# Windowed attention with sinks, then a maxout FFN: order of first loads, two reordered stretches, and one more chunk transposed by DMA

## The chip, the cores and the metric

The kernel runs on one NeuronCore of a Trainium2 chip. The metric is the device time of one execution in microseconds (us); the time of a kernel is the median of several runs. Five engines run side by side, each with its own instruction order: TensorE (PE; its weight loads are shown as PEld), VectorE (DVE), ScalarE (ACT), GpSimd (POOL) and SyncE (SP), which here only issues DMAs. They wait for each other by semaphores.

## The reference

Inputs are q, k, v of shape (4, 8, 768, 64) = batch, heads, positions, head width. Attention is causal with a window of 128 positions, and the first four positions of each sequence (the sinks) can always be seen. The heads are joined to x of 3072 tokens by 512, and a feed-forward layer takes the largest of three products:

```python
keep = is_sink | in_window            # in_window: 0 <= query - key < 128; is_sink: key < 4
scores = np.where(keep, q @ k.T / 8, -1e9)
x = softmax(scores) @ v               # per batch and head, then heads joined: (3072, 512)
h = np.maximum(np.maximum(x @ w1, x @ w2), x @ w3)      # w1, w2, w3: (512, 768)
out = h @ w_out                                         # w_out: (768, 512)
```

Inputs and output are float32; the kernel computes in bfloat16 with float32 sums.

## The kernel before

The 3072 tokens are cut into 12 chunks of 256, three to a batch (`CPB` is 3). Chunks 0, 3, 6 and 9 begin a batch: they have no sinks outside their own window and so no sink products. One token of text such as `Fa3` is a step: a letter for the kind, a letter for which chunk, and an argument. `run` turns the texts into instructions in just this order, on all engines; nothing is reordered later. Each engine takes its own instructions in the order in which they were written. The kinds that matter here:

- `K`, `Q`: k or q of a chunk is transposed on TensorE (`prep`, L227; `prep_runs`, L240, for chunks 1 and 2) and copied out of PSUM, k by VectorE, q mostly by ScalarE. From chunk 4 on this is done by the DMA crossbar instead: `D` (`turn`, L262) puts two transposing DMAs on SP's queue, and `E` (`place_k`, L221) lays out k on VectorE.
- `L` loads a chunk's q, k and v through SP's queue (L59, L89); GpSimd casts them to bfloat16 (`cast`, L215).
- `S` (L291) makes the scores of one pair of heads on TensorE and the exponentials on ScalarE; `M` (L314) multiplies by the mask on VectorE. `B` opens score buffers for chunks 0 and 1. `Z` (L321) makes the scores of the sinks, `V` (L337) opens a chunk's four attention outputs with the sinks' share, `A` (L349) adds the window's share for one pair of heads, and VectorE normalises it into x.
- `T` (`xpose`, L371) turns one half of a chunk's x into xT: up to chunk 4 by four transposes on TensorE and a copy, from chunk 5 on by one DMA on SP's queue.
- `F` (`ffn_h`, L389) makes one of nine groups of h on TensorE: eight matmuls of 256 columns, then a ScalarE copy (the groups 0, 3, 6, first weight) or a VectorE maximum (the others). `Y` and `W` (`ffn_y`, L410) make the output of a half or of a whole chunk; ScalarE copies it out of PSUM and SP stores it.

All PSUM tiles come from one pool of eight buffers with one tag, so that each new tile takes over the buffer of an older one and waits for its last reader. The masks, the sink rows and a few small matmuls for warming (`warm`, L124) are set up first. `sink_v_init` (L178) is four GpSimd instructions, two memsets and two copies, which prepare constants for the sinks' v rows. The first weights come by GpSimd's DMA queue (`load_runs`, `load_v`, `load_w`, `load_wo`), those of chunk 0 by SP's.

Chunks 0 to 2 and the beginning of chunk 3 are written out by hand (L501 to L546). Then a loop over chunks (L548) writes one pass for each: the h groups of chunk i, with the attention of chunk i+1 between them, the turning of chunk i+3 and the load of chunk i+4, then the scores of chunk i+2 and the output of chunk i. The passes of chunks 2 and 3 had texts of their own; in chunk 2's pass the output is made inside it (`Ya0`, `Ya1`) and the `Wa0` at the end is left out.

Of the kernel before, what the change touches and what calls it, by code (L numbers as in the profile page):

```python
# [16 lines left out]
def kernel(  # L17
# [24 lines left out]
    CPB = S // 256  # L42
# [8 lines left out]
    with tc.manual_schedule():  # L51
# [26 lines left out]
        def load_runs(ci):  # L78

            b, c = divmod(ci, CPB)  # L80
            t0 = c * 256
            runs[ci] = raw.tile([128, 2, 16 * D], BF16, tag="runs", bufs=2, name="runs")
            for j, src in ((0, k), (1, q)):
                nc.gpsimd.dma_start(
                    out=runs[ci][:, j],
                    in_=src[b, :, t0:t0 + 256].rearrange("h (r x) d -> h r (x d)", x=16))
            raws[ci] = [None]
# [10 lines left out]
        def load(ci, gate=None):  # L98
            load_qk(ci, gate)
            load_v(ci)  # L100
# [23 lines left out]
        def warm(n):  # L124

            wp = psum.tile([128, 128], F32, tag="f", name="warm")
            for _ in range(n):
                nc.tensor.matmul(wp, lhsT=ident, rhs=ident, start=True, stop=True)  # L128
# [29 lines left out]
        def load_w(wi, lo=0, hi=d_ff):  # L158

            w = (moe_w1, moe_w2, moe_w3)[wi]  # L160
            wt = const.tile([128, DS, hi - lo], BF16, name=f"w{wi}_{lo}")
            nc.gpsimd.dma_start(out=wt, in_=w[:, lo:hi].rearrange("(a p) f -> p a f", p=128))
            for fb in range(lo // 128, hi // 128):
                w_sb[wi, fb] = wt[:, :, fb * 128 - lo:fb * 128 - lo + 128]
# [3 lines left out]
        def load_wo():  # L168
            for a in range(2):
                nc.gpsimd.dma_start(  # L170
                    out=wo[:, 3 * a:3 * a + 3],
                    in_=moe_w_out[384 * a:384 * a + 384].rearrange("(a p) f -> p a f", p=128))
# [5 lines left out]
        def sink_v_init():  # L178
            nc.gpsimd.memset(sel, 0.0)
            nc.gpsimd.memset(v_sink[:, :, D:D + 1], 1.0)  # L180
            idv = ident[0:R, 0:R].rearrange("r (s p h) -> r p s h", p=NP, h=2)
            for h in range(2):
                nc.gpsimd.tensor_copy(sel[:, h, :, 0:2 * n_sink].rearrange(
                    "r p (s h) -> r p s h", h=2)[:, :, :, h], idv[:, :, :, h])

        def sink_v():
            for h in range(2):
                pv = psum.tile([128, B, D + 1], F32, tag="f", name="vs_ps")
                nc.tensor.matmul(pv, lhsT=sel[:, h].rearrange("r p x -> r (p x)"), rhs=v_sink,
                                 start=True, stop=True)  # L190
                nc.vector.tensor_copy(vs[:, :, h], pv)
# [3 lines left out]
        def cast_qk(ci, j, g, eng):  # L195
            if ci not in bfs:
                bfs[ci] = raw.tile([128, 2, 2, 2, 256], BF16, tag="qk_bf", name="qk_bf")
            src = raws[ci][0][:, j, g].rearrange("p (h i d) -> p h i d", h=4, d=D)
            if ci <= CPB:
                dst = bfs[ci][:, j, g]  # L200
            else:
                dst = bfs[ci][:, j].rearrange("p i a x -> p i (a x)")[:, :, 256 * g:256 * g + 256]
            (eng.tensor_copy if eng else nc.scalar.copy)(  # L203
                dst.rearrange("p i (h d) -> p h i d", d=D), src)
# [10 lines left out]
        def cast(ci):  # L215
            for j, g in ((0, 0), (1, 0), (0, 1), (1, 1)):
                cast_qk(ci, j, g, nc.gpsimd)
            for n in range(2):
                cast_v(ci, n, nc.gpsimd)
# [151 lines left out]
        def xpose(ci, t):  # L371
            if t == 0:
                xTs[ci] = work.tile([128, 2, DS, 128], BF16, tag="xT", bufs=3, name="xT")
            if ci > CPB + 1:
                nc.sync.dma_start_transpose(
                    out=xTs[ci][:, t], in_=xs[ci][:, t].rearrange("p h d -> p (h d)"))
                return
            pt = psum.tile([128, DS, 128], BF16, tag="f", name="xt_ps")
            x = xs[ci][:, t].rearrange("p h d -> p (h d)")
            for ds in range(DS):  # L380
                nc.tensor.transpose(pt[:, ds], x[:, ds * 128:(ds + 1) * 128], ident)  # L381
            copy = nc.vector.tensor_copy if ci == 0 else nc.scalar.copy
            copy(xTs[ci][:, t], pt)  # L383
# [69 lines left out]
        def step(op):  # L453

            name, ci, arg = op[0], int(op[1:3]), op[3:]
            if ci >= NCH:
                return
            if name in "KQ":
                (prep_runs if ci in runs else prep)(ci, int(name == "Q"), int(arg))
            elif name == "D":  # L460
                turn(ci)
            elif name == "L":
                load(ci)
            elif name == "E":
                place_k(ci, kTs.pop(ci), slice(0, NP))
            elif name == "S":
                score(ci, [int(x) for x in arg])
            elif name == "B":
                score_banks(ci, [int(x) for x in arg])
            elif name == "M":  # L470
                mask(ci, [int(x) for x in arg])
            elif name == "Z":
                if ci % CPB:
                    sink_score(ci)
            elif name == "X":
                if ci % CPB == 0:
                    sink_k(ci // CPB)
            elif name == "V":
                if ci % CPB:
                    sink_av(ci)  # L480
            elif name == "A":
                av(ci, int(arg))
            elif name == "T":
                xpose(ci, int(arg))
            elif name == "F":
                ffn_h(ci, int(arg))
            elif name == "Y":
                ffn_y(ci, [int(arg)], [range(FB)])
            elif name == "W" and ci == NCH - 1:
                ffn_y_end(ci)  # L490
            elif name == "W":
                ffn_y(ci, [0, 1], [range(4), range(4, FB)])

        def run(text, **at):
            for tok in text.split():
                c = at[tok[1]]
                step(f"{tok[0]}{c:02d}{tok[2:]}")

        sink_v_init()  # L501
        load_runs(1)
        load_v(1, nc.gpsimd)
        load_w(0, 0, 256)
        load_w(0, 256, d_ff)
        warm(36)
        cast_qk(0, 0, 0, nc.vector)
        cast_qk(0, 1, 0, nc.vector)
# [18 lines left out]
        load_runs(2)  # L527
        load_v(2, nc.gpsimd)
        load_wo()
        warm(3)  # L530
        run("Aa0 Aa1 Aa2 Aa3 Kb0 Qb0 Ta0 Ta1 Bb01 Sb01 Zb", a=0, b=1)
        sink_v()
        run("Bb23 Sb23 Fa0 Vb Ab0 Ab1 Fa3 Ab2 Ab3 Fa6 Fa1 Tb0 Tb1 Fa4", a=0, b=1)
        cast_v(2, 0, nc.gpsimd)
# [3 lines left out]
            a=0, b=1, c=2)  # L538
# [1 line left out]
        nc.gpsimd.memset(ve[1][:, :, :, D:D + 1], 1.0)  # L540
        cast(3)
        load(4)
        run("Fb5 Sc23 Mc23 Vc Ac0 Fb8 Ac1 Ya0 Ya1", a=0, b=1, c=2)
        cast(4)
        run("Ac2 Ac3 Yb0 Tc0 Tc1 Kd0 Qd0 Yb1 Kd1 Qd1", b=1, c=2, d=3)
        run("Zd Sd0123 Md0123 De Lf", d=3, e=4, f=5)  # L546

        for i in range(2, NCH):  # L548
            if i + 3 < NCH:
                cast(i + 3)  # L550
            text = "Fa0 Fa1 {} Fa2 {} Zc Sc0123 Mc0123 Wa0"
            if i == 2:
                text = text.format("", "Vb Ab0 Fa3 Ab1 Xb Fa4 Ab2 Fa5 Ab3 Fa6 Dd Le Fa7 Fa8 Ya0 Ec Tb0 Tb1 Ya1")
                text = text.replace(" Wa0", "")
            elif i == CPB:
                text = text.format("Ec", "Fa3 Vb Ab0 Fa4 Ab1 Fa5 Ab2 Fa6 Ab3 Dd Le Fa7 Fa8 Tb0 Tb1")
            elif i < 0:
                text = text.format("Ec", "Vb Ab0 Fa3 Xb Ab1 Fa4 Ab2 Fa5 Ab3 Fa6 Dd Le Fa7 Tb0 Tb1 Fa8")
            else:
                text = text.format("Ec", "Vb Ab0 Fa3 Xb Ab1 Fa4 Ab2 Fa5 Ab3 Tb0 Tb1 Fa6 Dd Le Fa7 Fa8")  # L560
            run(text, a=i, b=i + 1, c=i + 2, d=i + 3, e=i + 4)
# [38 lines left out]
```

## Time and profile before

| | |
|---|---|
| median of 7 runs | 183.31 us (182.16 to 183.87) |
| the profiled execution | 182.86 us, of which the span on the engines is 180.8 us |
| TensorE busy | 170.4 us (94% of the span) |
| VectorE, ScalarE, GpSimd busy | 115.5, 90.2, 69.8 us |
| moved by DMA | 33.63 MB, mean 186 GB/s |
| granted TensorE clock | 1.00 |
| DMA issues of xT on SP's queue | 14, median 2.9 us from issue to landing |
| of kT and qT on SP's queue | 8 each, 4.0 and 3.2 us |

The profile is one execution recorded by the hardware. All its times are microseconds from the beginning of the span, and it names tiles as the program does (`h_ps` is h in PSUM, `y_ps` the output, `o_ps` the attention output, `st` scores, `sk` sink scores, `xt_ps` transposed x). A line of it gives the line of the program, the engine, the operation, and output <- inputs with their shapes. In the timeline a bracket at the end tells how long the engine had been idle before and what released it. The chain of waits follows the work that ended last backwards through whatever released it. Matmul durations include the depth of a pipeline, so the sum of the busy times of single matmuls is more than what they add to the engine's sequence.

### The profile page before, as it was taken

How to read it: one execution, taken by the hardware profiler on the slowest of the kernel's cores; microseconds unless marked ns; L12 is line 12 of the kernel's file. 1: busy time of each engine (PE TensorE's matmuls, PEld its weight loads, DVE VectorE, ACT ScalarE, POOL GpSimd, SP SyncE). 2: the span in 40 equal slices, each digit the busy share in tenths (PEclk: the TensorE clock that was granted, in tenths of full speed). 3: DMA queues.
4: the chain of work that ended last, by engine and by line, in shares of the span. 5: the costliest groups of instructions: out<-in, count | busy, mean ns of one | idle time of the engine just before them, and what ended most of it. 6: DMA issues, size and time to landing. Idle time of an engine off the chain costs nothing.

```text
span 180.8 us, 4873 instructions
## 1 busy us (share of the span) xinstructions
PE 170.4 (94%) x1974; PEld 131.6 (73%) x1985; DVE 115.5 (64%) x245; ACT 90.2 (50%) x191; POOL 69.8 (39%) x121
## 2 busy tenths in 40 slices
PE   6869989999999999999999999999999999999991
PEld 6545878775697688588598687686796795796880
DVE  1686435687289189577667686687695776663451
ACT  2447742572981871951933924915636627522220
POOL 7985700657902294655025225426145300000001
PEclk9999999999999999999999999999999999999999
DMA  5999999999598999992789899897999625222404
GB/s 147 230 191 201 207 208 246 210 278 293 148 175 236 198 236 328 203 306 70 141 238 280 147 250 263 164 299 196 131 288 248 132 82 62 50 70 58 116 0 116
DMA packets 64645, 33.63 MB, mean 186 GB/s; under 512 B 26640, under 2 KB 60944, under 8 KB 64624
## 3 DMA queue, kind: packets, MB, share of 16 engines
q1 hardware_dynamic: 59520, 27.70, 65.6%
q0 software_dynamic: 4864, 5.38, 16.6%
q10 hardware_dynamic: 240, 0.26, 0.6%
q8 instruction: 15, 0.25, 0.5%
q14 instruction: 6, 0.05, 0.1%
HBM read 25.20 MB, written 6.29 MB: 174 GB/s over the span
## 4 chain that ended last, share of the span: by engine, by line
PE 76%; DMA 9%; ACT 5%; SPq 2%; issue 2%; DVE 2%; POOL 1%; POOLq 0%; ACTq 0%
PE h_ps L396 49%; PE y_ps L417 15%; DMA w<-in_moe_w_dram 7%; PE o_ps L358 5%; ACT e_sb L312 4%; DMA vs_raw<-in_v_dram 2%; PE st L306 2%; PE y_ps L436 2%; DVE h_sb L402 1%; SPq L70 1%; PE o_ps L345 1%; SPq L110 1%; PE sk L325 1%; PE xt_ps L381 1%; PE pt L251 1%
## 5 line engine op out<-in xcount | busy, mean ns | idle before, releaser
L396 PE MATMUL h_ps<-xT,w 128*128 128x256 bf16 x864 | 103.4, 273 | 1.2 <-DMA w<-in_moe_w_dram 0.8
L396 PEld LDWEIGHTS <-w 128*128 128x128 bf16 x864 | 81.1, 98 | 13.0 <-issue 1.7
L402 DVE TENSOR_TENSOR h_sb<-h_sb,h_ps 128x512 bf16<-128x512 bf16 x72 | 49.0, 683 | 27.7 <-PE h_ps L396 23.0
L312 ACT ACTIVATE e_sb<-st 128x512 bf16<-128x512 f32 (+1 forms) x96 | 45.3, 596 | 7.2 <-PE st L306 7.2
L400 ACT CAST h_sb<-h_ps 128x512 bf16<-128x512 f32 x36 | 22.0, 615 | 46.6 <-PE h_ps L396 46.6
L203 POOL CAST qk_bf<-qk_raw 128x512 bf16<-128x512 f32 x36 | 22.5, 631 | 47.7 <-DMA qk_raw<-in_k_dram 29.0
L319 DVE TENSOR_TENSOR e_sb<-e_sb,msk 128x1024 bf16<-128x1024 bf16 (+1 forms) x40 | 28.0, 706 | 18.7 <-ACT e_sb L312 18.5
L212 POOL CAST ve<-v_raw 64x512 bf16<-64x512 f32 x44 | 30.6, 694 | 23.8 <-DMA v_raw<-in_v_dram 21.0
L417 PE MATMUL y_ps<-wo,h_sb 128*128 128x512 bf16 x121 | 30.1, 379 | 0.9
L417 PEld LDWEIGHTS <-h_sb 128*128 128x128 bf16 x132 | 12.4, 97 | 14.1 <-issue 1.1
L366 DVE TENSOR_TENSOR x_sb<-o_ps,rc 128x256 bf16<-128x256 f32 x48 | 20.4, 424 | 1.6
L358 PE MATMUL o_ps<-ve,e_sb 128*128 128x65 bf16 x352 | 17.8, 193 | 0.9 <-DVE ve L212 0.9
L358 PEld LDWEIGHTS <-e_sb 128*128 128x128 bf16 x352 | 15.7, 97 | 3.0 <-issue 0.8
L423 ACT COPY y_sb<-y_ps 128x512 f32<-128x512 f32 x22 | 12.6, 635 | 9.8 <-PE y_ps L417 9.7
L306 PE MATMUL st<-qT,kk 64*128 64x128 bf16 (+1 forms) x256 | 13.5, 237 | 0.5 <-ACT qT L236 0.3
L407 POOL DMA_DIRECT2D out_dram<-y_sb x1 | 0.6, 571 | 34.5 <-ACT y_sb L447 34.5
L306 PEld LDWEIGHTS <-kk 64*128 64x128 bf16 x256 | 8.8, 94 | 4.7 <-issue 2.7
L363 DVE RECIPROCAL rc<-o_ps 128x4 f32<-128x4 f32 x48 | 8.4, 175 | 4.4 <-PE o_ps L358 4.2
L330 ACT ACTIVATE e_sink<-sk 128x256 bf16<-128x256 f32 x8 | 3.2, 395 | 5.6 <-PE sk L325 5.6
L128 PE MATMUL warm<-ident 128*128 128x128 bf16 x43 | 4.5, 286 | 1.4 <-POOL ident masks.py:199 1.4
L256 ACT CAST qT<-pt 128x512 bf16<-128x512 f32 x4 | 2.1, 588 | 7.2 <-PE pt L251 7.2
L383 ACT COPY xT<-xt_ps 128x512 bf16<-128x512 bf16 x8 | 4.3, 594 | 2.1 <-PE xt_ps L381 2.1
(58 smaller groups left out, 75.5 us busy)
## 6 DMA issues: line engine op xcount, KB each, us to landing
out_dram<-y_sb SPq DMA_DIRECT2D x22, 256.0 KB, 4.4
qk_raw<-in_k_dram SPq DMA_DIRECT2D x20, 256.0 KB, 4.3
qk_raw<-in_q_dram SPq DMA_DIRECT2D x20, 256.0 KB, 5.0
v_raw<-in_v_dram SPq DMA_DIRECT2D x10, 512.0 KB, 6.6
v_raw<-in_v_dram POOLq DMA_DIRECT2D x2, 512.0 KB, 10.3
w<-in_moe_w_dram POOLq DMA_DIRECT2D x2, 512.0 KB, 11.6
w<-in_moe_w_dram POOLq DMA_DIRECT2D x1, 768.0 KB, 15.1
wo<-in_moe_w_out_dram POOLq DMA_DIRECT2D x2, 384.0 KB, 14.3
```

Of the source, the lines that this page charges most:

```text
L203: (eng.tensor_copy if eng else nc.scalar.copy)(dst.rearrange("p i (h d) -> p h i d", d=D), src)
L212: (eng.tensor_copy if eng else nc.scalar.copy)(dst[64 * i:64 * i + 64], src[64 * n:64 * n + 64, :, i])
L306: nc.tensor.matmul(st[h][:, sl], lhsT=kx[r, p, k0:k0 + 128], rhs=qx[r], start=ci >= 2, stop=True, skip_group_check=ci < 2)
L312: nc.scalar.activation(e[:, h, lo:], st[:, lo:], AF.Exp, scale=scale)
L319: nc.vector.tensor_tensor(out=e, in0=e, in1=m, op=ALU.mult)
L358: nc.tensor.matmul(o[:, t, h], lhsT=es[ci, p][:, h, sl], rhs=ve[b % 2][:, n, 2 * p + h], start=(c == 0 and x == 0), stop=(x == len(blocks) ...
L366: nc.vector.tensor_mul(xs[ci][:, :, 2 * p:2 * p + 2], o[:, :, :, 0:D], rc.unsqueeze(3).to_broadcast([128, 2, 2, D]))
L396: nc.tensor.matmul(hp[:, f], lhsT=w_sb[wi, 2 * fp + f][:, ds], rhs=xTs[ci][:, :, ds], start=(ds == 0), stop=(ds == DS - 1))
L400: nc.scalar.copy(dst, hp)
L402: nc.vector.tensor_max(dst, dst, hp)
L417: nc.tensor.matmul(yps[ci, t], lhsT=hs[ci][:, fb, t * 128:(t + 1) * 128], rhs=wo[:, fb], start=(fb == 0), stop=(fb == FB - 1))
L423: nc.scalar.copy(y[:, t], yps.pop((ci, t)))
```

## The change

Six places are touched.

- `sink_v_init` is called after the five loads of chunk 1's runs and v and of the first weight, not before them.
- The 3 warming matmuls ahead of chunk 0's attention become 8, and another 8 come behind it, ahead of `Kb0`.
- `Fb8`, an h group of chunk 1, goes ahead of `Vc Ac0`, the sink share and first window share of chunk 2.
- `Yb1`, the second half of chunk 1's output, goes behind `Kd1 Qd1`, the second half of chunk 3's transposes.
- `xpose` uses the DMA for chunk 4 too.
- Chunk 3's pass of the loop takes the text of the later passes: the sink share and first window share come ahead of `Fa3` and each window share one h group sooner, and `Tb0 Tb1`, now DMAs on SP's queue, come ahead of `Fa6 Dd Le`, not at the end. (Its `Xb` does nothing for chunk 4. The text for `i < 0` was never used.)

```diff
         def xpose(ci, t):
             if t == 0:
                 xTs[ci] = work.tile([128, 2, DS, 128], BF16, tag="xT", bufs=3, name="xT")
-            if ci > CPB + 1:
+            if ci > CPB:
                 nc.sync.dma_start_transpose(
                     out=xTs[ci][:, t], in_=xs[ci][:, t].rearrange("p h d -> p (h d)"))
                 return
...
-        sink_v_init()
         load_runs(1)
         load_v(1, nc.gpsimd)
         load_w(0, 0, 256)
         load_w(0, 256, d_ff)
+        sink_v_init()
         warm(36)
...
-        warm(3)
-        run("Aa0 Aa1 Aa2 Aa3 Kb0 Qb0 Ta0 Ta1 Bb01 Sb01 Zb", a=0, b=1)
+        warm(8)
+        run("Aa0 Aa1 Aa2 Aa3", a=0)
+        warm(8)
+        run("Kb0 Qb0 Ta0 Ta1 Bb01 Sb01 Zb", a=0, b=1)
...
-        run("Fb5 Sc23 Mc23 Vc Ac0 Fb8 Ac1 Ya0 Ya1", a=0, b=1, c=2)
+        run("Fb5 Sc23 Mc23 Fb8 Vc Ac0 Ac1 Ya0 Ya1", a=0, b=1, c=2)
         cast(4)
-        run("Ac2 Ac3 Yb0 Tc0 Tc1 Kd0 Qd0 Yb1 Kd1 Qd1", b=1, c=2, d=3)
+        run("Ac2 Ac3 Yb0 Tc0 Tc1 Kd0 Qd0 Kd1 Qd1 Yb1", b=1, c=2, d=3)
...
-            elif i == CPB:
-                text = text.format("Ec", "Fa3 Vb Ab0 Fa4 Ab1 Fa5 Ab2 Fa6 Ab3 Dd Le Fa7 Fa8 Tb0 Tb1")
-            elif i < 0:
-                text = text.format("Ec", "Vb Ab0 Fa3 Xb Ab1 Fa4 Ab2 Fa5 Ab3 Fa6 Dd Le Fa7 Tb0 Tb1 Fa8")
             else:
                 text = text.format("Ec", "Vb Ab0 Fa3 Xb Ab1 Fa4 Ab2 Fa5 Ab3 Tb0 Tb1 Fa6 Dd Le Fa7 Fa8")
```

## The prediction

> **What bounds the kernel now.** I read the page's first two parts, then the chain of waits in order of time, then the timeline at the places that the diff touches, for all engines and for SP's queue alone.
>
> ```profile
> PE 170.4 (94%) x1974; PEld 131.6 (73%) x1985; DVE 115.5 (64%) x245; ACT 90.2 (50%) x191; POOL 69.8 (39%) x121
> PE   6869989999999999999999999999999999999991
> DMA  5999999999598999992789899897999625222404
> ```
>
> TensorE bounds it: after 27 us (slice 6) every slice but the last is at nine tenths. So a saving counts only if it shortens TensorE's own sequence or a gap in it. The gaps are in the first 24 us and at the hand-written places between chunks. The DMA engines are busy from 2 us on, so a sooner transfer takes its time from another one.
>
> The chain, at those places:
>
> ```profile
> 11.64 12.45 DMA w<-in_moe_w_dram
> 24.14 7.16 PE h_ps L396 x64
> ...
> 47.54 0.58 ACT y_sb L423
> 48.12 0.50 ACT qT L236
> 48.66 0.51 PE st L306 x8
> ...
> 71.77 0.45 PE xt_ps L381 x8
> ...
> 76.68 2.62 PE h_ps L396 x24
> ...
> 102.27 2.62 PE h_ps L396 x24
> ...
> 115.41 2.62 PE h_ps L396 x24
> ```
>
> The columns are start, length, what. The second half of w2's load lands at 24.09 (w2 is the program's wi=1). Near 48 us the scores hang on two ScalarE copies in a row. Chunk 3's pass of the loop lasts from 62.45 to 76.68 = 14.23 us; the pass of chunk 6, of the same kind, lasts 13.14 (102.27 to 115.41). What TensorE really loses stands in the brackets of the timeline (idle before, releaser):
>
> ```profile
> 5.72 0.76 POOL L84 DMA_DIRECT2D runs<-in_k_dram  x1
> 9.53 0.51 POOL L520 CAST v_sink<-vs_raw 32x256 bf16<-32x256 f32 x1
> 24.14 6.07 PE L396 MATMUL h_ps<-xT,w 128*128 128x256 bf16 x54 [0.82 <-DMA w<-in_moe_w_dram]
> ...
> 39.07 0.38 PE L345 MATMUL o_ps<-vs,e_sink 32*128 32x130 bf16 x6 [0.25 <-DVE h_sb L402]
> 48.66 0.51 PE L306 MATMUL st<-qT,kk 64*128 64x256 bf16 x8 [0.28 <-ACT qT L236]
> 71.16 0.42 DVE L366 TENSOR_TENSOR x_sb<-o_ps,rc 128x256 bf16<-128x256 f32 x1
> 71.50 1.47 DVE L402 TENSOR_TENSOR h_sb<-h_sb,h_ps 128x512 bf16<-128x512 bf16 x2
> ```
>
> **The change part by part.**
>
> *Sooner DMA issue.* `sink_v_init` (two memsets, two copies) holds GpSimd from 4.89 to 5.72. Behind it come five DMA issues: two of chunk 1's runs, its v, two of the first weight. They go 0.83 us sooner. The four instructions then run from 8.70 to 9.53, and the cast of v_sink starts at 9.53 as now (its input landed at 9.19). So w2's loads are still issued at 10.90. They can land sooner only because the queue ahead of them is further on: each of GpSimd's loads lands right behind the one before (v of chunk 1 at 15.3, the first weight at 16.6 and 19.5, w2 at 20.9 and 24.1).
>
> How much of the 0.83 us arrives? The row speaks for all of it, since this queue is in order and never empty. A rule of the Trainium skill speaks against ("DMA: Bandwidth & Descriptors", "Queues, rings and completion order"): each DMA engine serves the queues that have work in turn, packet by packet, so a sooner queue takes from SP's loads of chunk 0 and adds no bandwidth. By the rule only idle engines count. By stretches of 1 us the DMA share is 0.9 to 1.1 from 3 to 8 us, then 0.59 from 8 to 9, then 1.0 and more: the gain would be about 0.4 us. I take 0.5, between 0.4 and 0.83. The cap is TensorE's idle 0.82. Lower end: chunk 0's v lands later (now about 9.1). VectorE is busy nearly throughout from 9.13 to 15.7, so it passes most of such a delay on. It has 0.82 us of cover at 24.14, and cannot be much over the 0.83 us taken from SP, so the part ends near 0 or at -0.1.
>
> *Warm-up matmuls.* Three become eight, and eight are added behind the first attention products: 13 small matmuls at some 0.055 us (three took 0.34 with the pipeline's latency). The first five end by 10.4, where TensorE waits for v's cast until 10.38 and again until 11.31. The other eight, 0.45 us, stand between 12.1 and 12.55. `Kb0` then ends near 13.0 and `Qb0` starts there, where it now starts at 13.17 after a wait of 0.44 for q. Cost: nothing, under the waits for v and q. Without that cover it is 0.45 us, and the 0.82 us before 24.14 takes it up first.
>
> *`Fb8` ahead of `Vc Ac0`.* From 36.19 to 40.78 TensorE's sequence lasts 4.59 us; its pieces add up to 3.99 (two h groups 1.75, scores 0.56, sink 0.22, two attention products 0.35 and 0.24, h 0.87). 0.60 is lost, the bulk before the sink products at 39.07: their PSUM buffers are freed by VectorE's maxima (37.75 to 39.62, three in a row). `Fb8` is 0.87 us of work whose buffer comes from the first of these maxima, ready at 38.4. The sink products then start near 39.5 and wait perhaps 0.1 for the last maximum. Gain 0.4, between 0.1 and 0.6. On VectorE `Fb8`'s maximum (0.68) goes ahead of chunk 2's normalisation, which nobody needs before the transposes at 45; the 1.29 us of `Yb0` lie between.
>
> *`Yb1` behind `Kd1 Qd1`.* The chain charges 1.08 us (0.58 + 0.50), but TensorE stood idle for only 0.28 before `st`: that is the gain. With the change, ScalarE's copy of q ends near 48.0 and the scores for it come at 48.4, behind six matmuls. ScalarE's copy of y goes from 47.54 to about 48.0; the exponentials start at 48.6 in both orders. SP's store of y goes 0.46 later, and behind it chunk 4's transposes (49.49) and the load of chunk 5 (53.77): their users come at 58.5 and 57.2. The latter is a GpSimd wait of 7.55 us that ends when the data come; what it feeds is first used at 60.2. Gain 0.25, between 0 and 0.3.
>
> *Chunk 4 transposed by DMA, and chunk 3's pass ordered as the later ones.* Removed: eight transposes (0.45 us of TensorE) and two ScalarE copies (2 x 0.59) at 72. The rest of the gap to 14.23 is waits that these copies lengthen. From above, the gain is that to chunk 6's pass, 1.09 us. From the pieces: 72 h groups' matmuls 7.86, sink 0.23, attention 1.07, sink scores 0.22, scores 0.99, y 2.75 = 13.12. But chunk 3's pass differs in one thing: its y was taken forward, so VectorE's masks and maxima pile up, and it is busy without a gap from 66.58 to 72.97. The last maxima free the buffers of the last scores, as now. Scores end near 73.3, y takes 2.75, and chunk 4's h group starts at 76.05: gain 0.63. A second wait is added: the sink products now come before `Fa3` and their fourth buffer is freed by the seventh exponential near 65.4, against 65.1 on TensorE. That 0.3 us vanishes in VectorE's backlog. I take 0.6.
>
> The new transposes on SP: x of chunk 4 is ready at 71.58 (71.16 + 0.42), so they issue at 71.65 and 72.9. The fourteen on record land 2.9 us after issue (2.4 to 4.4). With 2.9 it is 75.8, 0.25 us before TensorE asks; with 4.4 it is 77.3, and then the stage loses 0.6 against now. Queued behind them on SP: chunk 6's two transposes (now 69.61 and 71.62) go to 74.15, its kT lands 3.2 to 4.7 later, by 78.9, and VectorE asks for it near 78.5. The load of chunk 7 goes from 73.72 to 76.8; it is cast by about 84, before SP turns chunk 7 at 86. Stores of y come later still (78.31). None sets TensorE's time, with under 1 us to spare at kT.
>
> Sum: 0.5 + 0 + 0.4 + 0.25 + 0.6 = 1.75 us. The profiled execution of 182.86 (span 180.8) becomes 181.1, and the median of the runs, 183.31, becomes about 181.5. Afterwards TensorE's passes of 12.6 to 13.1 us are as before, only sooner.
>
> **The rivals.**
> - *The transfer is hidden anyway:* DMA engines are full at the start and w2 lands at 24.1 as now. For: shares of 0.9 to 1.1. Against: the stretch of 0.59. Gain 1.25, time 182.05.
> - *A new wait for the one removed:* chunk 4's xT lands with the slowest latency, TensorE waits until 77.3. For: the margin is 0.25 us. Against: SP's earlier loads are nearly in by 72 (0.26 share at 73 to 74). Gain 0.5 + 0.4 + 0.25 - 0.6 = 0.55, time 182.75.
> - *Slower:* the same place, worse: the two transposes share the engines with chunk 6's load and more of SP's work. The end is over 0.5% later only if chunk 4's h group starts past 78.8 (76.68 + 1.15 of other gains + 0.92), 7.2 us after x; then 184.4 or so. The longest pair on record would make 6.1.
> - *More than forecast:* the pass falls to chunk 6's 13.14 and w2 comes a full 0.82 sooner: 2.6 us, time 180.7.
>
> **How the numbers follow.** Forecast 0.55, hidden transfer 0.12, late xT 0.13, slower 0.08, more 0.12. About 0.5% (0.92 us; the seven runs spread over 182.16 to 183.87) is what can be told from no change: the border is 182.39. Of the forecast nearly all lies below it, with the upside and a part of the hidden transfer: 0.70. The late xT and the rest: 0.21. Slower 0.09. The range from 180.4 to 182.9 reaches from the upside to the late xT.
>
> **What would show it.** Right: GpSimd's first load issued at 4.9; the wait for w2 at 24.14 gone or under 0.4; no idle before L345 and L306 near 39 and 48; in chunk 3's pass no xt_ps and about 13.6 us. Wrong: an idle TensorE before L396 with the releaser DMA xT near 76, VectorE waiting for kT, or chunk 0's v cast later than 9.5.

## The result, and the profile after

The median of the kernel before is 183.2 us over 31 runs, that of the changed kernel 181.25 us over 12 (180.40 to 181.81). The ratio is 0.990, with a 95% interval from 0.9877 to 0.9924: about 1.8 us or 1% faster. 181.5 (180.4 to 182.9) had been predicted. The profiled execution took 180.4 us, span 178.6, against 182.86 and 180.8. Not all of the gain lies in this span: the device time is 2.06 us longer than the span in the kernel before, 1.83 in the changed kernel, each within 0.08 us in every execution on record. So about 0.23 of the 1.95 us between the medians was won outside what the profile shows, by a cause that no run isolates.

The page of the changed kernel, parts 1 and 2:

```profile
PE 170.9 (96%) x1978; PEld 132.1 (74%) x1990; DVE 117.4 (66%) x245; ACT 89.2 (50%) x189; POOL 71.6 (40%) x121
PE   6979999999999999999999999999999999999991
DMA  5999999999599889889999897896999923222404
```

TensorE's busy time stays at 170 to 171 us while the span loses 2.2 us: what went is idle time. In the row of slices the second, third and sixth rise by a tenth each (8 to 9, 6 to 7, 8 to 9), all in the first 27 us. The later gaps, of about 0.3 us in a slice of 4.5, don't show. Where the time went is read from the start of the same work in the chain of waits (start, length, what):

```profile
4.70 7.88 DMA runs<-in_k_dram
12.62 1.20 PE pt L251 x64
...
61.00 2.78 PE h_ps L396 x24
...
74.64 2.62 PE h_ps L396 x24
...
100.31 2.68 PE h_ps L396 x24
...
113.51 2.62 PE h_ps L396 x24
```

The load of w2 (`11.64 12.45` before) is no longer in the chain. A DMA has taken its place: the keys of chunk 1, issued at 4.70, landed after 7.88 us. Further down, the h groups of chunks 3, 4, 6 and 7 start 1.45, 2.04, 1.96 and 1.90 us sooner than at 62.45, 76.68, 102.27 and 115.41. All but 0.6 us has been won by chunk 3, and from chunk 4 on nothing is added until near the end.

The timeline of the changed kernel, at the places that the prediction named (the bracket is the idle time before, and its releaser):

```profile
4.70 0.76 POOL L84 DMA_DIRECT2D runs<-in_k_dram  x1
12.52 0.39 POOL L520 CAST v_sink<-vs_raw 32x256 bf16<-32x256 f32 x1 [3.28 <-DMA vs_raw<-in_v_dram]
12.62 1.20 PE L251 MATMUL pt<-ident,runs 128*64 128x64 bf16 x64 [0.42 <-DMA runs<-in_k_dram]
...
23.10 1.05 PE L396 MATMUL h_ps<-xT,w 128*128 128x256 bf16 x8
...
38.71 0.30 PE L345 MATMUL o_ps<-vs,e_sink 32*128 32x130 bf16 x8
46.53 1.06 PE L306 MATMUL st<-qT,kk 64*128 64x256 bf16 x16
...
69.71 0.42 DVE L366 TENSOR_TENSOR x_sb<-o_ps,rc 128x256 bf16<-128x256 f32 x1
70.20 2.53 SPq L375 DMA_TRANSPOSE xT<-x_sb  x2
...
74.48 1.69 PE L396 MATMUL h_ps<-xT,w 128*128 128x256 bf16 x14
```

Three brackets are gone: the 0.82 for w2 before the h group (now at 23.10), the 0.25 before the sink products (38.71), the 0.28 before the scores (46.53). Chunk 4's transposes are DMAs now, and its first h group at 74.48 has no bracket: they landed in time. Two brackets are new, both at the start: 0.42 before chunk 1's keys on TensorE, and 3.28 on GpSimd, which waits for `vs_raw` until 12.5. The first has only taken the place of an older one, before chunk 1's queries:

```profile
13.17 0.69 PE L251 MATMUL pt<-ident,runs 128*64 128x64 bf16 x32 [0.44 <-DMA runs<-in_q_dram]
```

Before, these transposes ended at 13.86 (13.17 + 0.69); now all 64 end at 13.82 (12.62 + 1.20). So the later keys cost TensorE nothing here.

The passes of chunks 2 and 3 before begin and end with these lines (the first h groups of chunks 2, 3 and 4):

```profile
49.10 2.79 PE L396 MATMUL h_ps<-xT,w 128*128 128x256 bf16 x24
62.45 3.65 PE L396 MATMUL h_ps<-xT,w 128*128 128x256 bf16 x32
76.52 2.78 PE L396 MATMUL h_ps<-xT,w 128*128 128x256 bf16 x24
```

By stage, in us, from the timelines of the two profiled executions:

| work | before | after | won in this stage | predicted |
|---|---|---|---|---|
| chunk 2's key transposes on TensorE | 31.23 | 30.36 | 0.87 (sooner DMA issue) | 0.5 |
| chunk 2's first h group | 49.10 | 47.67 | 0.56 (`Fb8`, `Yb1`) | 0.65 |
| chunk 3's first h group | 62.45 | 61.00 | 0.02 | 0 |
| chunk 4's first h group | 76.52 | 74.48 | 0.59 (chunk 3's pass) | 0.6 |
| the passes of chunks 4 and 5 | | | -0.14 | 0 |
| chunk 9's pass | 13.53 | 13.14 | 0.39 | 0 |

At the start, single profiles of kernels that are alike there differ by more than a microsecond (1.5 and 1.8 us, given below), so the first row needs the experiments most.

### The profile page after: what moved, and what is told of

It is laid out like the page before. It is cut to its first block, busy times and chain, and to the rows that moved or that the text cites. A ratio compares the mean times of both kernels' runs of the same rounds, so it can differ in the third digit from the quotient of the medians.

```text
span 178.6 us, 4886 instructions
## 1 busy us (share of the span) xinstructions
PE 170.9 (96%) x1978; PEld 132.1 (74%) x1990; DVE 117.4 (66%) x245; ACT 89.2 (50%) x189; POOL 71.6 (40%) x121
## 4 chain that ended last, share of the span: by engine, by line
PE 88%; DMA 4%; POOL 2%; ACT 2%; DVE 1%; issue 1%; POOLq 0%; ACTq 0%
PE h_ps L396 54%; PE y_ps L417 16%; PE o_ps L358 6%; DMA runs<-in_k_dram 4%; PE st L306 4%; PE y_ps L436 2%; PE pt L251 1%; ACT e_sb L312 1%; PE o_ps L345 1%; PE xt_ps L381 1%; PE sk L325 1%; PE st L288 1%; DVE h_sb L402 1%; POOL msk L139 1%; PE pt L233 1%
## 5 line engine op out<-in xcount | busy, mean ns | idle before, releaser
L319 DVE TENSOR_TENSOR e_sb<-e_sb,msk 128x1024 bf16<-128x1024 bf16 (+1 forms) x40 | 30.2, 762 | 17.5 <-ACT e_sb L312 16.9
L212 POOL CAST ve<-v_raw 64x512 bf16<-64x512 f32 x44 | 32.5, 740 | 22.0 <-DMA v_raw<-in_v_dram 20.1
L203 POOL CAST qk_bf<-qk_raw 128x512 bf16<-128x512 f32 x36 | 23.0, 644 | 41.5 <-DMA qk_raw<-in_k_dram 31.8
L423 ACT COPY y_sb<-y_ps 128x512 f32<-128x512 f32 x22 | 12.5, 632 | 9.3 <-PE y_ps L417 9.2
L128 PE MATMUL warm<-ident 128*128 128x128 bf16 x56 | 5.9, 287 | 1.4 <-POOL ident masks.py:199 1.4
L128 PEld LDWEIGHTS <-ident 128*128 128x128 bf16 x56 | 5.1, 134 | 1.6 <-POOL ident masks.py:199 1.4
## 6 DMA issues: line engine op xcount, KB each, us to landing
w<-in_moe_w_dram POOLq DMA_DIRECT2D x1, 768.0 KB, 12.5
```

What stands on the lines that cost most here:

```text
L203: (eng.tensor_copy if eng else nc.scalar.copy)(dst.rearrange("p i (h d) -> p h i d", d=D), src)
L212: (eng.tensor_copy if eng else nc.scalar.copy)(dst[64 * i:64 * i + 64], src[64 * n:64 * n + 64, :, i])
L319: nc.vector.tensor_tensor(out=e, in0=e, in1=m, op=ALU.mult)
L423: nc.scalar.copy(y[:, t], yps.pop((ci, t)))
```

## The experiments

*The theory* is the prediction's: each of three parts takes away a wait of TensorE where it says (start, the two reordered texts, chunk 3's pass with the DMA transposes), and the parts add up. *The rivals:* that the new text of chunk 3's pass alone brings its gain and the crossbar nothing; that the crossbar's gain is taken back by what is queued behind it; that the start is worth nothing, since its transfers only change places; and that the warming matmuls, costed at zero, are what helps. The kernels fall into three sets, in each of which they were compared with the kernel before on one chip; the ratios are to that kernel, with 95% intervals.

**Only `sink_v_init` moved** (the kernel before, and this):

```diff
-        sink_v_init()
         load_runs(1)
         ...
         load_w(0, 256, d_ff)
+        sink_v_init()
```

> Only the move of sink_v_init behind the five loads, all else as before. My theory: TensorE's idle before the second half of w2 (0.82 us in the profile before) goes, so the time falls by 0.4 to 0.9 us (ratio 0.995 to 0.998), with the cast of v_sink on GpSimd held up by its small load from SP and w2 issued later than before without harm. Rival (the transfer is hidden, the DMA engines are full): w2 lands at 24 us as before and the time is unchanged, ratio 1.000 within 0.001.

Measured: 0.9997 (0.9963 to 1.0032). The profiled execution (span 180.0) shows what came sooner and what came later:

```profile
12.60 1.20 PE L251 MATMUL pt<-ident,runs 128*64 128x64 bf16 x64 [0.93 <-DMA runs<-in_k_dram]
12.68 0.39 POOL L520 CAST v_sink<-vs_raw 32x256 bf16<-32x256 f32 x1 [3.17 <-DMA vs_raw<-in_v_dram]
13.63 0.75 POOL L162 DMA_DIRECT2D w<-in_moe_w_dram  x1
```

The wait of 0.82 for w2 is gone, and 0.93 for chunk 1's keys has come, in place of the 0.44 for its queries: the 64 transposes end at 13.80, where they had ended at 13.86. The keys were issued a microsecond sooner and landed 1.3 us later than before (12.6 against 11.3). `vs_raw`, last among SP's small loads, landed at 12.6 where it had landed at 9.19. Neither delay held TensorE up in this execution. So the part has its effect in its records (chunk 2's keys at 30.34 for 31.23), yet no gain that the times can tell: at most some 0.7 us, by the interval.

**Only the two texts of chunks 1 to 3 reordered:**

```diff
-"Fb5 Sc23 Mc23 Vc Ac0 Fb8 Ac1 Ya0 Ya1"
+"Fb5 Sc23 Mc23 Fb8 Vc Ac0 Ac1 Ya0 Ya1"
-"Ac2 Ac3 Yb0 Tc0 Tc1 Kd0 Qd0 Yb1 Kd1 Qd1"
+"Ac2 Ac3 Yb0 Tc0 Tc1 Kd0 Qd0 Kd1 Qd1 Yb1"
```

> Only the two reordered texts, Fb8 ahead of Vc Ac0 and Yb1 behind Kd1 Qd1. My theory: what counts is TensorE's idle time, so 0.47 and 0.16 us go as in the changed kernel's profile, in sum 0.6 us, ratio 0.9965. Rival: what counts is the share of the chain of waits, 1.08 us for the two ScalarE copies alone, so 1.3 us or more, ratio 0.993.

Measured: 0.996 (0.9939 to 0.9981), that is 0.73 us. In its trace the stretch from chunk 2's key transposes to its first h group is 17.31 us, as in the changed kernel:

```profile
31.89 0.70 PE L251 MATMUL pt<-ident,runs 128*64 128x64 bf16 x32
49.20 2.78 PE L396 MATMUL h_ps<-xT,w 128*128 128x256 bf16 x24
```

Before it is 17.87, from this line to the 49.10 above:

```profile
31.23 0.70 PE L251 MATMUL pt<-ident,runs 128*64 128x64 bf16 x32
```

So 0.56 us is won in the place that was predicted (0.65). This part is faster on its own. But its device time is only 1.71 us longer than its span, for 2.06 before: some 0.35 of the 0.73 us falls outside the span, where no wait of TensorE is. Between the spans the difference of the means is 0.4 us.

**Only chunk 4 by DMA, with the later passes' text for chunk 3:**

```diff
-            if ci > CPB + 1:
+            if ci > CPB:
...
-            elif i == CPB:
-                text = text.format("Ec", "Fa3 Vb Ab0 ... Fa8 Tb0 Tb1")
```

> Only chunk 4: x transposed by DMA and chunk 3's pass with the text of the later passes. My theory: chunk 3's pass (14.23 us from its first h group to the next chunk's) falls to about 13.65, time down by 0.6 us, ratio 0.997. Rival (xT lands late): TensorE waits for the DMA near 76 us and the time is unchanged or up by 0.6 us, ratio 1.000 to 1.003. Rival from above: the pass falls to chunk 6's 13.14, 1.1 us, ratio 0.994.

Measured: 1.0029 (1.0007 to 1.0052). Chunk 3's pass fell from 14.07 to 13.51 us, as predicted; and the next pass, of chunk 4, rose from 12.96 to 13.92, which gives it back and more. (This kernel too ends 0.35 us nearer to its span: between the spans it is 0.8 us slower.) The timeline of this kernel at the end of that pass:

```profile
83.03 3.07 SPq L375 DMA_TRANSPOSE xT<-x_sb  x2
...
87.85 1.07 ACT L423 COPY y_sb<-y_ps 128x512 f32<-128x512 f32 x2
89.00 1.00 PEld L396 LDWEIGHTS <-w 128*128 128x128 bf16 x10 [1.26 <-DMA xT<-x_sb]
89.03 1.14 PE L396 MATMUL h_ps<-xT,w 128*128 128x256 bf16 x9 [0.79 <-ACT y_sb L423]
```

TensorE waits for chunk 5's xT. (The matmuls' bracket names a copy of y. The weight load ahead of them, released at the same moment, names the DMA, and before the change chunk 5's h group started while those copies were still running.) Chunk 5's two transposes landed 5.2 and 4.6 us after their issue, the second at 88.9; before the change that one took 2.5. What the DMA engines did meanwhile, by stretches of 1 us, in this kernel:

```profile
83.00:84.00 1.00, 1.00 (x12) 0.90 (x10) 0.32 (x1) 0.32 (x1) 0.47 (x1) 1.00 1.13 363
84.00:85.00 1.00, 1.00 (x18) 0.67 (x16) 0.89 (x2) 0.25 (x1) 0.14 (x1) 1.00 1.27 376
```

and in the kernel before:

```profile
83.00:84.00 1.00, 1.00 (x17) 0.91 (x14) 0.97 (x4) 0.00 (x0) 0.91 (x2) 1.00 0.01 2
84.00:85.00 1.00, 1.00 (x11) 0.90 (x10) 0.35 (x1) 0.58 (x1) 0.93 (x2) 1.00 0.00 0
```

The last two columns are the engines' share and GB/s. Before, the load of chunk 7, issued at 73.72, was in by then and the engines stood still. Here it was issued at 76.63, behind the transposes of chunks 4 and 6 on SP's queue, and was still coming in at 363 to 376 GB/s when chunk 5's transposes were issued.

**Only the warming matmuls** (3 become 8, and 8 more ahead of `Kb0`):

```diff
-        warm(3)
-        run("Aa0 Aa1 Aa2 Aa3 Kb0 Qb0 ...
+        warm(8)
+        run("Aa0 Aa1 Aa2 Aa3", a=0)
+        warm(8)
+        run("Kb0 Qb0 ...
```

> Only the warming matmuls: 3 become 8, and 8 more behind the first attention products. My theory: they lie under waits for v and for chunk 1's q, and 0.82 us of idle time for w2 would take up what is left, so the time is unchanged, ratio 1.000 within 0.001. Rival 1: they stand on the path, plus 0.45 us, ratio 1.0025. Rival 2: they keep TensorE at full pace, minus 0.3 us or more with shorter spacing of the matmuls between 10 and 24 us.

Measured: 0.9986 (0.9964 to 1.0008): no difference, as costed.

**The whole change once more**, in a second set, beside three kernels that each take one part out of it.

> The changed kernel unaltered, so that the next three have it beside them on the same chip: ratio 0.990, within 0.988 to 0.992. In the records of single parts the sum is only -0.3% (0.9997, 0.996, 1.0029, 0.9986); if the parts simply added up, it would be 0.997.

Measured: 0.9897 (0.9848 to 0.9946). The passes of chunks 3, 4 and 5 are 13.47, 13.16 and 12.81 us, where the kernel before has 14.07, 12.96 and 12.63: of 0.60 won, 0.38 is given back in the two passes behind it.

**The change without its chunk 4 part:**

```diff
-            if ci > CPB:
+            if ci > CPB + 1:
...
+            elif i == CPB:
+                text = text.format("Ec", "Fa3 Vb Ab0 ... Fa8 Tb0 Tb1")
```

> The changed kernel without its chunk-4 part (x of chunk 4 by TensorE again, chunk 3's pass with its old text). Theory 1 (the part is worth its 0.6 us inside the whole change; alone it lost it again because chunk 7's load ran into chunk 5's transposes): 0.6 us slower than the changed kernel, ratio 0.993. Theory 2 (the part costs, as alone): faster than the changed kernel by 0.3%, ratio 0.987.

Measured: 0.9869 (0.9834 to 0.9905), median 180.9 us. It is at least as fast as the whole change: passes 14.07, 12.96 and 12.63 again, and nothing lost in the sum. The intervals overlap, so that it is faster is not shown; that the chunk 4 part brings 0.6 us of time is not seen either.

**The change without the sooner issue:**

```diff
+        sink_v_init()
         load_runs(1)
         ...
         load_w(0, 256, d_ff)
-        sink_v_init()
```

> The changed kernel with sink_v_init ahead of the five loads again. Theory 1 (the sooner issue brings w2 about 0.8 us sooner): 0.4 to 0.9 us slower than the changed kernel, ratio 0.992 to 0.995, with idle before the h group at 23 to 24 us. Theory 2 (the landing of w2 varies by itself from execution to execution, alone the part gave nothing): ratio 0.990 as the changed kernel.

Measured: 0.9889 (0.9847 to 0.9932), as the whole change. In its profile the wait for w2 is back, and costs 0.61:

```profile
24.01 1.16 PE L396 MATMUL h_ps<-xT,w 128*128 128x256 bf16 x9 [0.61 <-DMA w<-in_moe_w_dram]
```

Over all profiles, the five with the old order at the start have chunk 2's key transposes at 31.06 us on average (30.41 to 31.89; waits for w2 of 0 to 1.28), the other nine at 30.56 (29.95 to 31.73; no wait for w2 in any). That is a difference of 0.5 between means, in spreads of 1.5 and 1.8.

**The change without its added warming matmuls:**

```diff
-        warm(8)
-        run("Aa0 Aa1 Aa2 Aa3", a=0)
-        warm(8)
-        run("Kb0 Qb0 ...
+        warm(3)
+        run("Aa0 Aa1 Aa2 Aa3 Kb0 Qb0 ...
```

> The changed kernel with 3 warming matmuls as before. Theory 1 (hidden and without effect): ratio 0.990, within 0.001. Theory 2 (they are what keeps TensorE at pace, -0.14% alone): slower by 0.3 us or more, ratio 0.992 or higher, with wider spacing of the matmuls from 10 to 24 us. Theory 3 (they are on the path): faster by 0.45 us, ratio 0.9875.

Measured: 0.9947 (0.9922 to 0.9972). That seemed to speak for the warming. The profiled execution shows other losses:

```profile
14.49 0.69 PE L251 MATMUL pt<-ident,runs 128*64 128x64 bf16 x32 [1.59 <-DMA runs<-in_q_dram]
```

TensorE waited 1.59 us for the queries of chunk 1, and 0.56 us for the xT of chunk 5. Warming matmuls use no data of either transfer. But this is one execution of 22, of 183.37 us where the median is 182.52, and it doesn't account for the ratio. So the warming was taken out altogether in a third set.

**The change without any warming at either place** (the `warm(3)` of the kernel before left out as well):

```diff
-        warm(8)
         run("Aa0 Aa1 Aa2 Aa3", a=0)
-        warm(8)
```

> The changed kernel without the 8 and 8 warming matmuls around chunk 0's attention (none at either place). Theory 1 (they keep the granted clock up; so far it was under 0.993 in none of 52 executions with 16 of them and in 26 of 147 with 3): the share of executions under 0.993 is at least that of 3 matmuls, so some 4 or more of 20, and the time is 0.3 to 0.7% over the changed kernel's, ratio 0.993 to 0.997. Theory 2 (the 26 are chance or another part's doing): no execution under 0.993 and ratio 0.990.

Measured: 0.9882 (0.9837 to 0.9928): as the whole change. With 16 matmuls and with none the time is the same to within about 1 us; why the kernel with 3 is slower than both stays open.

**The change with chunk 4 still transposed on TensorE, at the new place in the text** (`ci > CPB` back to `ci > CPB + 1`, nothing else):

> The changed kernel with x of chunk 4 transposed by TensorE again, but at the new place in chunk 3's pass (behind Ab3, ahead of Fa6). Theory 1 (the crossbar takes the gain back, because its transposes push chunk 7's load on SP's queue into chunk 5's transposes; the order is what shortens the pass): pass 3 (first h group of chunk 3 to that of chunk 4) about 13.6 us against 13.48 with the DMA and 14.07 before, pass 4 at 12.96 as before, time at or under the changed kernel's, ratio 0.986 to 0.988. Theory 2 (the crossbar is what shortens the pass): pass 3 near 13.9 to 14.0, ratio 0.989 or higher.

Measured: 1.0019 (0.9994 to 1.0044). Chunk 3's pass takes 16.08 us, 2 us more than in the kernel before. TensorE and VectorE in the timeline:

```profile
68.66 0.36 PE L381 MATMUL xt_ps<-ident,x_sb 128*128 128x128 bf16 x2
69.94 0.23 PE L381 MATMUL xt_ps<-ident,x_sb 128*128 128x128 bf16 x1 [0.92 <-DVE x_sb L366]
71.08 0.45 PE L381 MATMUL xt_ps<-ident,x_sb 128*128 128x128 bf16 x5 [0.92 <-DVE x_sb L366]
```

```profile
68.65 0.68 DVE L402 TENSOR_TENSOR h_sb<-h_sb,h_ps 128x512 bf16<-128x512 bf16 x1
...
69.45 0.42 DVE L366 TENSOR_TENSOR x_sb<-o_ps,rc 128x256 bf16<-128x256 f32 x1
69.80 0.68 DVE L402 TENSOR_TENSOR h_sb<-h_sb,h_ps 128x512 bf16<-128x512 bf16 x1
...
70.60 0.42 DVE L366 TENSOR_TENSOR x_sb<-o_ps,rc 128x256 bf16<-128x256 f32 x1
```

VectorE is behind by several operations and makes the last pieces of x at 69.45 and 70.60. A transpose on TensorE must wait there, and all h groups behind it wait with it. A transpose on SP's queue waits just as long, but nothing of TensorE is queued behind it. So in this pass the new text alone is worth -2 us, and with the crossbar +0.6. The crossbar with the old text, its transposes at the end of the pass, was not run.

**A trial of a better version:** the last kernel, its transposes of chunk 4 on TensorE, with the same earlier place for the transposes in chunk 2's pass:

```diff
-"... Fa5 Ab3 Fa6 Dd Le Fa7 Fa8 Ya0 Ec Tb0 Tb1 Ya1"
+"... Fa5 Ab3 Tb0 Tb1 Fa6 Dd Le Fa7 Fa8 Ya0 Ec Ya1"
```

> A candidate: the changed kernel with chunk 4's x transposed by TensorE at the new place, as g1_pe_T, and chunk 3's transposes in chunk 2's pass also moved from the end to the place behind Ab3. My theory: in pass 2 (13.33 us, its pieces 12.87) the scores no longer wait behind ScalarE's two copies of xT, so it falls to 12.9 to 13.1; with g1_pe_T's gain the ratio is 0.984 to 0.986. Rival: the exponentials hold TensorE at the same point anyway (0.61 us before the first h group in all profiles), pass 2 stays at 13.3 and the ratio is g1_pe_T's.

Measured: 1.0112 (1.0064 to 1.0161), slower, for the reason just shown: chunk 2's pass takes 15.28 us for 13.35, with this in it:

```profile
54.55 0.23 PE L381 MATMUL xt_ps<-ident,x_sb 128*128 128x128 bf16 x1 [0.68 <-DVE x_sb L366]
55.70 0.45 PE L381 MATMUL xt_ps<-ident,x_sb 128*128 128x128 bf16 x5 [0.92 <-DVE x_sb L366]
```

**Is it the late load of chunk 7 that makes chunk 5's transposes late?** The change without its chunk 4 part, with that load held back by a wait on ScalarE:

```diff
-Ab3 Dd Le Fa7
+Ab3 Dd Fa7
+                text = text.replace("Mc0123", "Ge Mc0123")
...
+            elif name == "G":
+                load(ci, nc.scalar)
```

> The changed kernel without its chunk-4 part (as f2_no_chunk4, ratio 0.987), but chunk 7's load is held back by a one-element ScalarE copy behind the exponentials of chunk 3's pass, so that it is issued some 1 us behind chunk 4's first h group, where the change puts it, and not 2.8 us ahead. No crossbar transpose of chunk 4. Theory 1 (the late load is what costs): pass 4 (12.96) grows by 0.1 to 0.9 us through late transposes of chunk 5, and the time by 0.2 to 0.4%, ratio 0.989 to 0.991. Theory 2 (something else of the chunk-4 part costs): pass 4 stays at 12.96, ratio 0.987.

Measured: 0.9886 (0.9854 to 0.9918). The load is issued at 75.69, later than in the changed kernel (75.52), and chunk 4's pass loses nothing:

```profile
75.69 0.39 SPq L70 DMA_DIRECT2D qk_raw<-in_k_dram  x1
...
82.56 2.53 SPq L375 DMA_TRANSPOSE xT<-x_sb  x2
```

The second of chunk 5's transposes landed 2.5 us after issue, and chunk 4's pass took 12.96. It landed 1.30 us before chunk 5's h group began, as in all eight profiles of kernels without the chunk 4 part (1.30 to 1.31). In the six with it 0.14 was left in four, among them the changed kernel, and 0.49 and 0.95 in the others. In those four the h group waited for xT: at every wait for it in these profiles 0.14 us lies between the landing and the first matmul. So with the chunk 4 part this margin shrinks or is used up, and the late load alone leaves it as it was.

The next pass, of chunk 5, lost something all the same: it took 12.81 us for 12.63, for chunk 6's xT landed at 100.30, 4.0 us after issue, and the h group began at 100.43:

```profile
100.40 2.53 PEld L396 LDWEIGHTS <-w 128*128 128x128 bf16 x24 [0.48 <-issue]
100.43 2.78 PE L396 MATMUL h_ps<-xT,w 128*128 128x256 bf16 x24
```

Whether the late load has a part in that isn't shown: in the other kernels without the chunk 4 part, which load chunk 7 sooner, this margin is anything from 0.14 to 1.35 us. The data of the load came in by 84.1, those of the changed kernel's by 85.0. What makes chunk 5's transposes late (the transposes of chunks 4 and 6 directly ahead of the load, when all come together, or the 0.9 us by which it ends later) stays open.

## Why the prediction was right

*The sum.* 1.75 us was forecast, and the medians differ by 1.95, some 0.23 of it outside the span. That the sum came out so well is in part luck. The waits went where the prediction said, in the profiles; but of its terms only the 0.65 for the two texts is seen in the times of a part alone, the 0.5 is not resolved, and the 0.6 is given back, in part or wholly, in the two passes behind it in most profiles that have it.

*Sooner issue, 0.5.* The step is seen in the records, though in wide spreads: 0.87 in the profiled pair and 0.50 between the means of all profiles; the wait for w2 is gone in all nine kernels that have it. Two parts of the working failed. The prediction had w2's loads issued at 10.90 as before, since `vs_raw` had landed at 9.19. It landed at 12.5, and w2 was issued at 13.48. That w2 came in by 23.05 all the same says that the issue was never what it waited for: the queue ahead of it was. And the price was put on chunk 0's v. That landed at 9.08 for 9.01; `vs_raw` (3.3 us later) and chunk 1's keys came late instead, and TensorE passed on neither delay. The rule that the prediction weighed, the Trainium skill's "DMA: Bandwidth & Descriptors", "Queues, rings and completion order", by which each DMA engine takes the queues that have work in turn, fits what is seen: from 8 to 9 us the DMA share went from 0.59 to 0.94, which the rule's lower value of 0.4 counted on, and beyond that, transfers changed places. The gain itself, 0.87 or 0.50, doesn't decide between that 0.4 and the 0.83 of the row. In the times the part is not resolved: 0.9997 alone, and 0.9889 for the change without it.

*Warming, 0.* Nothing against it in its own run (0.26 us faster, give or take 0.4) and in the one without any; the slower kernel with 3 is left unexplained.

*`Fb8` and `Yb1`, 0.65.* Right: the stretch that holds them takes 17.84 to 17.88 us in the four profiles with the old texts, 17.3 to 17.4 in eight of ten with the new ones. The other two have 17.58 and 17.72; in the latter, the repeat, the sink products wait again, 0.21 us for VectorE, where the prediction had put "perhaps 0.1". In the times of that part alone 0.73 was won, half of it outside the span. It is the only part whose gain stands outside the interval on its own.

*Chunk 3's pass, 0.6.* Right in its place (0.59) and in its reason. (The prediction's 14.23 took both ends from the chain, where a piece starts only when the one before has ended; from the timeline the pass was 14.07.) That VectorE's backlog makes x late is what the kernel with the transposes on TensorE shows, at the price of 2 us. The transposes were issued at 70.20 (71.65 forecast less the 1.45 by which all had come sooner), and landed in time in the changed kernel; the margin of 0.25 us was as thin as it looked, since in two other profiles the weight load ahead of the h group waited 0.35 and 0.40 for xT, and the pass grew by 0.03 and 0.13 (13.51 and 13.61 for 13.48). Nor is the gain in every profile: the change without any warming shows 13.98 for this pass, with 0.40 idle before scores whose buffer VectorE had not freed. What failed is the sentence "None sets TensorE's time": with the load of chunk 7 issued 1.8 us later, while all else came 2 us sooner, and more transposes ahead of it on the queue, the next chunk's transposes land later. That cost 1.24 us in one kernel, 0.38 in the repeat, 0.14 in the changed kernel, and with the part left out the kernel is no slower. The nearest thing in the prediction was the rival of a late xT, placed one chunk too soon.

*What has no step.* In the profile of before 0.39 us went in chunk 9's pass, at this wait:

```profile
154.34 2.53 PEld L396 LDWEIGHTS <-w 128*128 128x128 bf16 x24 [0.70 <-issue]
154.37 2.78 PE L396 MATMUL h_ps<-xT,w 128*128 128x256 bf16 x24 [0.23 <-ACT e_sb L312]
```

The bracket's name misleads. The DMA view of the second transpose of chunk 10, issued at 150.00, says what it was:

```profile
xT<-x_sb SPq DMA_TRANSPOSE x1, 4.2
```

It landed at 154.23, 0.14 us before the h group, the 0.14 of a wait for xT; in the changed kernel it took 3.1 us. In the kernels with one part each, two of four profiles have the same wait, 0.34 and 0.35 with xT's DMA as releaser, and two have none. The changed kernel has none there, nor have those that leave one part of it out. It is no effect of an edit near it; why this transpose takes 3 us at one time and over 4 at another, with no load running, single profiles don't say.

*What stays open.* The four parts one by one multiply to 0.9972, with about 0.005 either way. The whole is 0.990, with 0.0024. The remainder of 0.7% lies just outside of this. It is no matter of the clock: among the executions with a mean granted clock of 0.993 or more alone, the median spans of the four parts differ from the kernel before by -0.4, -0.4, +0.8 and -0.3 us, that of the whole in the second set by -1.4. Nor is it chunk 4's part: by the medians it costs 0.003 alone and as much in the whole (0.9897 against 0.9869). The waits for xT before the h groups of chunk 10 or 11, which the profiles of three single parts have and that of the whole has not, are a candidate for more, and not shown. Open too is the time outside the span: some 2.07 us in the kernel before and in those with only the issue or the warming changed, 1.84 with both the reordered texts and chunk 4 by DMA, 1.71 with one of these two.

## What to carry to other kernels

An engine that takes its work in order turns one late operand into a delay of everything behind it: the operation that waits belongs on a queue behind which nothing urgent stands. Moved forward there, the transposes brought the pass to 13.48 us; moved forward on TensorE, to 16.08. A transfer that is moved on a shared queue is to be followed to the next stage as well: the load behind it, and the transfers that meet that load, set what is left of the gain. At a start with the DMA engines nearly full, as here, expect of a sooner issue that it changes who goes first more than how much arrives; ask which small load at the end of another queue will come late, and whether anything waits for it. And compare the span of the profile with the device time before a gain in the times is put down to a wait in the profile.

## What the runs showed of the hardware

*The granted clock differs between executions of one kernel.* In most executions its mean is 0.995 to 1.0. In all 14 profiled ones that is the end alone: the record stands at 1.0 from 4 to 7 us on and at 0.5 from 2 us or more behind the last matmul, where it costs nothing. In some executions the mean is near 0.99 (below 0.993), and those are longer, by 1.0 to 2.7 us between the medians of their spans. With the 16 warming matmuls and no long wait of TensorE this was so in 0 of 58 executions; with 3 of them, the kernel before included, in 35 of 201; with none in 3 of 6 (median span 180.6 against 178.9 in the other three). In the kernels with transposes waiting for x in chunk 3's pass it was so in 16 of 28, in spite of the 16 matmuls. The Trainium skill's "TensorE: Matmul & The Clock Gate", "Part 1: The HAM clock gate (the "warmup" mystery)", has the clock halved after a window of some 3.4 us without work. One such window at half speed is, by that figure, an estimate of 1.7 us, 0.9% of 182 us and so a mean of 0.991; both are near what was measured. The same page's bound, under "Why this matters for your kernels", no idle gaps over about 3 us between bursts, is kept in all profiles: behind the start TensorE's longest wait is 1.59 us. But no profiled execution caught such a loss, so where it falls isn't shown, nor whether a longer wait stood there, nor that the matmuls prevent it.

*Small loads at the end of a busy queue.* With GpSimd's queue starting 0.8 to 1.1 us sooner, chunk 1's keys took 6.9 to 8.2 us from issue to landing in nine profiles, for 5.5 to 6.4 in the five with the old order. The cast that needs `vs_raw`, the last of SP's small loads, began at 10.4 to 12.7 us, for 9.4 to 10.7.

*Transposes by the crossbar.* The second of chunk 5's pair took 2.5 us from issue to landing in the kernel before, that of chunk 10 took 4.2 to 4.4 in three profiles, both with no load running; while a load came in at about 370 GB/s, chunk 5's pair took 5.2 and 4.6. A pair kept SP's queue 2.5 to 3.8 us.
